# Attention, three-way maximum and gated feed-forward on one Trainium2 core: where the SBUF tiles begin, modulo 128 bytes

## The chip, the cores and the metric

One core of one Trainium2 chip runs the whole program. The metric is device time in microseconds (us), the median of several executions. Before the change it is 1110.41 us, with three runs between 1109.85 and 1111.0.

## What is computed

Inputs are float32 q, k, v of shape [4, 12, 448, 64] and five weight matrices that arrive as 8-byte floats. The reference, cut to its arithmetic:

```python
scores = q @ k.transpose(0, 1, 3, 2) / sqrt(64)
scores = cap * tanh(scores / cap)
attn = softmax(scores)
x = (attn @ v), heads joined            # [1792, 768]
h = maximum(maximum(x @ w1, x @ w2), x @ w3)   # w1..w3 [768, 768]
y = h @ w_out                           # [768, 768]
out = (silu(y @ w_gate) * (y @ w_val)) @ wo    # [768, 1536] twice, [1536, 768]
```

## The kernel before

TensorE multiplies float32 in the reduced form `float32r`. To keep the accuracy, nearly every operand is cut into a high and a low part (`parts_of`, L507: ACT or POOL copies the high part, DVE or POOL subtracts), and every product is made of three matmuls: high by high, high by low, low by high. Each matmul loads its own 128 x 128 weights (the stationary operand) and streams 448 or 384 columns (the moving operand) through them. Moving columns are 4 bytes each, so one matmul reads 1792 or 1536 contiguous bytes from every partition.

The work goes through these stages; the names are those of the trace, written out<-in.

- Attention, pairs of heads: `scores` (L217, `sc<-qh,kh` and the like), `values` (L257). For the first eight pairs `values` multiplies plain float32 (`pv<-e,vp`, moving `e`), and the trace holds two records for each such matmul. Later pairs use the parts `eh`, `el`. Transposes of q and k (L193, L207) have the identity as their moving operand.
- `x @ w1..w3` (`ff1`, L566, and `group`, L551: `ps_h<-x,ws`, 1296 matmuls, moving `x`), woven into the attention of the next batch by `weave` (L594), then alone. Meanwhile the 8-byte weights are loaded (`raw`), turned into float32 by integer arithmetic (`convert`, L468) and cut into parts (`ws`, L514) in steps given out one by one.
- `h @ w_out` (`ps_y<-ha,ws`, 432 matmuls, moving `ha`).
- `y @ w_gate` and `y @ w_val` in seven products instead of eight (`product`, L871, 1512 matmuls). Half of the moving operands lie in `yo0` (in the trace `yo`), the other half in `b11`, `yo1a`, `yo1b`, `yo1c` (in the trace `b`, `yo1a`, ...).
- the last product (`out_part`, L942: `ps_o<-wo,g`, 1008 matmuls of 384 columns, moving `wo`).

The order of the work on each engine is written out by hand (`manual_schedule`); the change leaves it as it is. What concerns the change is the memory. SBUF pools stack up from two ends of each partition: those of the default side from low addresses up, those with `side="right"` from the top (byte 229344) down. `const` (L52) is the first pool of the left side, so what it holds shifts everything that is stacked on it: `cv`, `wp`, `per`, `stk`, `ring`, `seq`, `wo` and the rest. On the right side lie `res` (with `x`), `yo0`, `yf` and `ct`.

The first tile of `const`, `ident`, begins at byte 1152 = 9 x 128. Behind it stands `four` (L54), four columns of per-partition constants, 16 bytes that take 32. Nearly all other tiles are whole multiples of 128 bytes long (the largest: 1792 = 14 x 128, 2048, 3072, 3584, 6144, 10752, 21504, 73728, 75264). So before the change every large tile on the left begins at 32 past a multiple of 128, and every large tile on the right at 96 past one, because 229344 is 1791 x 128 + 96. The start of the operands in a partition, as the built program has them:

| tile | side | before, first byte | before, modulo 128 | after, first byte | after, modulo 128 |
|---|---|---|---|---|---|
| ident | left | 1152 | 0 | 1152 | 0 |
| qn, kn | left | 1696 | 32 | 1664 | 0 |
| ws, o_A, o_S, g (weights of matmuls) | left | 22176 | 32 | 22144 | 0 |
| e, eh, el | left | 87712 | 32 | 87680 | 0 |
| ha, yo1a | left | 66720 | 32 | 66688 | 0 |
| wo (moving) | left | 55968 | 32 | 55936 | 0 |
| x | right | 127456 | 96 | 127360 | 0 |
| yo0 | right | 154080 | 96 | 153984 | 0 |
| ct, yf | right | 132576 | 96 | 132480 | 0 |

Every slice that a matmul reads lies a whole multiple of 128 bytes into its tile, or, for some weights of `pv`, a multiple of 64 bytes.

Of the kernel before, what the change touches and what calls it, by code (L numbers as in the profile page):

```python
# [9 lines left out]
F32 = mybir.dt.float32  # L10
# [14 lines left out]
@with_exitstack  # L25
def attention_max_silu_kernel(ctx, tc, q, k, v, cap, w1, w2, w3, w_out, wg, wv, wo, out):

    nc = tc.nc
    B, H, S, D = q.shape
    P = 128
    CQ = S // 4
    KL = S - 3 * P
    NP = H // 2  # L50

    const = ctx.enter_context(tc.tile_pool(name="const", bufs=1))  # L52
    ident = const.tile([P, P], F32, name="ident")
    four = const.tile([P, 4], F32, name="four")  # L54
    capt, acap, ncap, qsc = (four[:, i : i + 1] for i in range(4))


    qn = [const.tile([P, 4, 2, D], F32, name=f"qn{i}") for i in range(2)]
    kn = [const.tile([P, 4, 2, D], F32, name=f"kn{i}") for i in range(2)]

    def load_pair(g):
        load_k(g)
        load_q(g)

    def load_k(g):
        b, hp = divmod(g, NP)
        load_keys(k[b, 2 * hp : 2 * hp + 2], kn[g % 2])

    def load_q(g):
        b, hp = divmod(g, NP)  # L70
        for j in range(2):
            (nc.scalar if g < NP + 2 else nc.sync).dma_start(
                out=qn[g % 2][:CQ, :, j], in_=q[b, 2 * hp + j].rearrange("(p c) d -> p c d", c=4)
            )

    def load_keys(src, t, outside=False):


        for j in range(2):
            r = slice(j * KL, (j + 1) * KL)  # L80
            nc.sync.dma_start(
                out=t[:, j, 0:3] if outside else t[:, 0:3, j],
                in_=src[j, : 3 * P].rearrange("(p c) d -> p c d", c=3),
            )
            nc.sync.dma_start(out=t[r, j, 3] if outside else t[r, 3, j], in_=src[j, 3 * P :])

    bits = nc.values_load(cap.rearrange("(a b) -> a b", a=1).bitcast(mybir.dt.int32))
    with tc.manual_schedule(), tc.tile_pool(name="ps_w", bufs=1, space=PSUM) as ps_w:
        nc.gpsimd.memset(kn[0][:, 3], 0.0)
        nc.gpsimd.memset(kn[1][:, 3], 0.0)  # L90
        make_identity(nc, ident)
        load_pair(0)
        nc.scalar.dma_start(out=capt, in_=cap.partition_broadcast(P))
        load_pair(1)
        nc.scalar.activation(qsc, ident[:, 0:1], AF.Tanh)
        ps = ps_w.tile([P, 512], F32, name="warm")
        for i in range(24):
            nc.tensor.transpose(ps[:, i % 4 * P : (i % 4 + 1) * P], ident, ident)  # L98

    shared = dict(ident=ident, capt=capt, acap=acap, ncap=ncap, qsc=qsc, qn=qn, kn=kn, load_k=load_k, load_q=load_q, load_keys=load_keys)  # L100
    tensors = (q, k, v, w1, w2, w3, w_out, wg, wv, wo, out)
    with tc.If((bits & 0x7FFFFFFF) < 0x42000000) as bounded:
        program(tc, tensors, shared, False)
    with bounded.Else():
        program(tc, tensors, shared, True)
# [955 lines left out]
```

## Time and profile before

| | |
|---|---|
| median of 3 runs | 1110.41 us (1109.85 to 1111.0) |
| the profiled execution: span from first to last instruction | 1111.6 us |
| PE (TensorE) busy | 1075.8 us, 97% |
| DVE, POOL, ACT busy | 685.2, 658.5, 511.9 us |
| mean share of the 16 DMA engines in use | 35.6% |
| mean granted TensorE clock | 0.988 of full speed |

The profiled execution's own time is given by its span, 1.2 us above the median. PE's busy time is the union of its matmuls' spans; since they overlap in the pipeline, a busy PE can still stream slower or faster. What a stream of matmuls costs is read from the distance between starts: n matmuls in a row that are listed with a length L, of which one lasts d, start (L - d)/(n - 1) apart.

### The profile page before, as it was taken

To read this page: it belongs to the slowest core of one execution; us is meant where nothing else is said; L and a number is where in the kernel's file an instruction comes from. 1 tells how busy PE (TensorE), PEld (TensorE's weight loads), DVE (VectorE), ACT (ScalarE), POOL (GpSimd) and SP (SyncE) were. 2 spreads that over 40 slices of the span, in tenths; PEclk is the share of its full clock that TensorE was granted. 3 is DMA by queue.
4 is the path that set the end of the run, shared out by engine and by line. 5 is a ranking of instruction groups with operands and counts; after the bars stand their busy time and mean duration, and the time that the engine had idled before them with its cause. 6 is when DMAs were issued, how large, how long until landed. Compare 5 with 4: busy or idle time off the path is not lost.

```text
span 1111.6 us, 15026 instructions
## 1 busy us (share of the span) xinstructions
PE 1075.8 (97%) x5480; PEld 937.4 (84%) x5480; DVE 685.2 (62%) x884; ACT 511.9 (46%) x798; POOL 658.5 (59%) x550
## 2 busy tenths in 40 slices
PE   7986999999999999999999999999999998999998
PEld 4443778888888888999998999999999998999997
DVE  2766899957777677866547876666667645211110
ACT  4766768867677664343535433333332233212110
POOL 1356998787887879997363456655655555211210
PEclk9999999999999999999999999999999998999999
DMA  5555445433434422433212023333233228232231
GB/s 140 132 140 157 116 114 146 115 100 104 137 93 116 132 91 94 151 117 126 95 46 82 17 75 105 98 111 101 91 95 117 68 84 250 66 108 86 85 100 61
DMA packets 158531, 118.44 MB, mean 107 GB/s; under 512 B 72432, under 2 KB 153840, under 8 KB 158448
## 3 DMA queue, kind: packets, MB, share of 16 engines
q1 hardware_dynamic: 150880, 115.55, 34.6%
q10 hardware_dynamic: 7568, 1.84, 0.7%
q8 instruction: 45, 0.74, 0.3%
q14 instruction: 38, 0.31, 0.1%
HBM read 90.44 MB, written 26.82 MB: 105 GB/s over the span
## 4 chain that ended last, share of the span: by engine, by line
PE 86%; DMA 4%; DVE 3%; POOL 2%; ACT 2%; SPq 1%; issue 1%; ACTq 0%; POOLq 0%; DVEq 0%
PE ps_g L880 28%; PE ps_h L558 23%; PE ps_o L952 16%; PE pv L278 7%; PE ps_y L558 5%; PE sc L229 5%; DMA rb<-rd 1%; DMA su<-o 1%; POOL yf L728 1%; PE pq L193 1%; PE pk L207 1%; DMA rd<-rs 1%; DVE el L253 1%; DMA hr<-h 1%; PE warm L98 0%
## 5 line engine op out<-in xcount | busy, mean ns | idle before, releaser
L558 PE MATMUL ps_h<-x,ws 128*128 128x448 f32 x1296 | 287.4, 368 | 0.7 <-ACT ht L581 0.7
L558 PEld LDWEIGHTS ps_h<-x,ws 128*128 128x128 f32 x1296 | 238.6, 188 | 35.2 <-issue 17.3
L512 POOL TENSOR_TENSOR ws<-w,ws 128x384 fp32r<-128x384 f32 x144 | 181.6, 1270 | 11.6 <-ACT ws L509 4.1
L952 PE MATMUL ps_o<-wo,g 128*128 128x384 f32 x1008 | 177.9, 338 | 3.7 <-ACT g L509 2.5
L952 PEld LDWEIGHTS ps_o<-wo,g 128*128 128x128 f32 x1008 | 177.3, 190 | 4.4 <-ACT g L509 2.8
L499 POOL TENSOR_TENSOR t<-t,raw 128x768 uint32<-128x768 uint32 x42 | 82.4, 1961 | 117.0 <-DVE raw L496 108.9
L253 DVE TENSOR_TENSOR el<-e,eh 128x896 fp32r<-128x896 f32 x64 | 88.0, 1378 | 43.6 <-ACT eh L252 36.3
L243 ACT ACTIVATE e<-e,four 128x896 f32<-128x896 f32 x96 | 99.4, 1035 | 4.8 <-DMA qn<-in_q_dram 3.9
L512 POOL TENSOR_TENSOR g<-gr,g 128x384 fp32r<-128x384 f32 x28 | 32.8, 1193 | 113.4 <-ACT g L509 113.4
L235 ACT ACTIVATE e<-sc,four 128x896 f32<-128x896 f32 x96 | 86.9, 905 | 23.0 <-PE sc L229 22.9
L880 PE MATMUL ps_g<-yo,o_S 128*128 128x448 f32 x432 | 93.5, 362 | 0.0
L558 PE MATMUL ps_y<-ha,ws 128*128 128x448 f32 x432 | 90.5, 371 | 3.1 <-ACT ha L509 1.5
L558 PEld LDWEIGHTS ps_y<-ha,ws 128*128 128x128 f32 x432 | 82.2, 191 | 11.4 <-ACT ha L509 1.8
L880 PEld LDWEIGHTS ps_g<-yo,o_S 128*128 128x128 f32 x432 | 81.0, 187 | 6.0
L278 PE MATMUL pv<-eh,vs 128*128 128x448 f32 (+1 forms) x256 | 76.9, 381 | 0.0
L511 POOL TENSOR_SCALAR ws<-w 128x384 fp32r<-128x384 f32 x90 | 76.2, 847 | 0.0
L512 DVE TENSOR_TENSOR g<-gr,g 128x384 fp32r<-128x384 f32 x28 | 24.9, 899 | 74.6 <-ACT g L509 74.5
L880 PE MATMUL ps_g<-yo,o_A 128*128 128x448 f32 x324 | 70.3, 362 | 0.0
L880 PEld LDWEIGHTS ps_g<-yo,o_A 128*128 128x128 f32 x324 | 60.8, 188 | 4.5
L904 ACT ACTIVATE ct<-ct 128x448 f32<-128x448 f32 x23 | 13.3, 579 | 99.4 <-DVE ct L903 99.4
L499 POOL TENSOR_TENSOR w<-w,raw 128x768 uint32<-128x768 uint32 x18 | 36.4, 2020 | 38.0 <-DVE raw L496 38.0
L278 PE MATMUL pv<-e,vp 128*128 128x448 f32 (+1 forms) x128 | 53.7, 592 | 3.9 <-ACT o L296 2.6
(135 smaller groups left out, 1872.2 us busy)
## 6 DMA issues: line engine op xcount, KB each, us to landing
raw<-in_moe_w_dram SPq DMA_DIRECT2D x18, 768.0 KB, 4.6
raw<-in_moe_w_out_dram SPq DMA_DIRECT2D x18, 768.0 KB, 4.8
gr<-gd SPq DMA_DIRECT2D x14, 768.0 KB, 5.2
raw<-in_moe_w_gate_dram SPq DMA_DIRECT2D x12, 768.0 KB, 4.7
raw<-in_moe_w_val_dram SPq DMA_DIRECT2D x12, 768.0 KB, 4.6
rb<-rd SPq DMA_DIRECT2D x48, 112.0 KB, 3.0
h<-ht SPq DMA_DIRECT2D x24, 224.0 KB, 2.0
hr<-h SPq DMA_DIRECT2D x24, 224.0 KB, 2.7
```

Source lines behind the costliest of these rows:

```text
L229: nc.tensor.matmul(ps[:, j, :S], a[r, cols_], m[r], start=i == 0, stop=i == 2)
L235: nc.scalar.activation(ee[n][:, :w], ps[:, :w, :S], AF.Tanh, scale=qsc)
L243: nc.scalar.activation(t, t, AF.Exp, bias=ncap, scale=acap)
L253: nc.vector.tensor_sub(lo, t, f(hi))
L278: nc.tensor.matmul(pv[g][j][:, :S], a, m, start=c == 0 and x == 0, stop=c == 3 and x == len(ops) - 1,)
L499: nc.gpsimd.tensor_tensor(t, t, low, op=ALU.add)
L511: copier.tensor_scalar(hi, src, 1.0, 1.0, ALU.mult, ALU.mult)
L512: subtracter.tensor_tensor(lo, src, f(hi), op=ALU.subtract)
L558: nc.tensor.matmul(ps, a, m, start=kk == 0 and n == 0, stop=kk == NK - 1 and n == 2)
L880: nc.tensor.matmul(ps, a[:, s0, k3], m[:, kk, s1], start=kk == 0 and j == 0, stop=kk == 2 and j == 2,)
L904: nc.scalar.activation(t[0], t[0], AF.Silu)
L952: nc.tensor.matmul(po[s][x][:, :HW], a, m[:, x * HW : (x + 1) * HW], start=c == 0 and n == 0, stop=c == NF2 - 1 and n == 2,)
```

## The change

`four` leaves the pool `const` and gets a pool of its own, `top`, the first on the right side, with 24 columns (96 bytes) instead of 4. The four columns that are used stay the first four. The 96 bytes reach from 229248 to the top, so that the pools below begin at 229248 = 1791 x 128; on the left `qn` follows `ident` directly. On every engine and every DMA queue the instructions, their order and their waits are the same as before, and so are the PSUM banks and the DRAM scratch tensors.

```diff
     const = ctx.enter_context(tc.tile_pool(name="const", bufs=1))
     ident = const.tile([P, P], F32, name="ident")
-    four = const.tile([P, 4], F32, name="four")
+    top = ctx.enter_context(tc.tile_pool(name="top", bufs=1, side="right"))
+    four = top.tile([P, 24], F32, name="four")
     capt, acap, ncap, qsc = (four[:, i : i + 1] for i in range(4))
```

## Rows read from the trace of the kernel before

**Rows 1.** The page's busy times by engine.
```profile
PE 1075.8 (97%) x5480; PEld 937.4 (84%) x5480; DVE 685.2 (62%) x884; ACT 511.9 (46%) x798; POOL 658.5 (59%) x550
```

**Rows 2.** The page's chain that ended last, by engine and by line.
```profile
PE 86%; DMA 4%; DVE 3%; POOL 2%; ACT 2%; SPq 1%; issue 1%; ACTq 0%; POOLq 0%; DVEq 0%
PE ps_g L880 28%; PE ps_h L558 23%; PE ps_o L952 16%; PE pv L278 7%; PE ps_y L558 5%; PE sc L229 5%; DMA rb<-rd 1%; DMA su<-o 1%; POOL yf L728 1%; PE pq L193 1%; PE pk L207 1%; DMA rd<-rs 1%; DVE el L253 1%; DMA hr<-h 1%; PE warm L98 0%
```

**Rows 3.** Windows by stage: length, busy us of each engine, granted clock, DMA share, GB/s.
```profile
175.00:425.00 250.00, 250.00 (x1336) 207.64 (x1335) 188.20 (x218) 177.65 (x231) 202.45 (x185) 1.00 0.38 113
425.00:525.00 100.00, 98.59 (x493) 91.09 (x492) 73.99 (x77) 38.99 (x78) 92.81 (x74) 1.00 0.37 119
525.00:608.00 83.00, 80.63 (x387) 73.56 (x386) 43.71 (x57) 39.03 (x74) 36.50 (x27) 0.98 0.26 84
608.00:935.00 327.00, 323.31 (x1579) 298.00 (x1579) 226.51 (x340) 110.74 (x207) 188.31 (x148) 0.99 0.30 95
935.00:1112.00 177.00, 171.31 (x988) 170.99 (x986) 30.06 (x41) 31.27 (x66) 33.67 (x27) 0.99 0.32 95
```

**Rows 4.** Timeline of PE, 690 to 698 us: start, us, instructions merged.
```profile
690.33 1.96 PE L880 MATMUL ps_g<-yo,o_S 128*128 128x448 f32 x9
692.13 2.02 PE L880 MATMUL ps_g<-yo1c,o_S 128*128 128x448 f32 x9
693.99 1.96 PE L880 MATMUL ps_g<-yo,o_A 128*128 128x448 f32 x9
```

**Rows 5.** Timelines of PE in four long runs of matmuls without a gap.
```profile
449.81 24.36 PE L558 MATMUL ps_h<-x,ws 128*128 128x448 f32 x121
...
540.74 20.23 PE L558 MATMUL ps_y<-ha,ws 128*128 128x448 f32 x99
...
603.69 8.63 PE L558 MATMUL ps_y<-ha,ws 128*128 128x448 f32 x41
...
955.69 140.56 PE L952 MATMUL ps_o<-wo,g 128*128 128x384 f32 x810
```

**Rows 6.** Groups by shape: busy us, mean ns of one, idle before.
```profile
L880 PE MATMUL ps_g<-yo,o_S 128*128 128x448 f32 x432 | 93.5, 362 | 0.0
...
L278 PE MATMUL pv<-eh,vs 128*128 128x448 f32 x192 | 63.4, 371 | 0.0
```

**Rows 7.** Timeline of PE near 40 us: plain float32, two passes; and one run of it.
```profile
39.60 1.29 PE L278 MATMUL pv<-e,vp 128*128 128x448 f32 x3
...
54.32 0.54 PE L278 MATMUL pv<-e,vp 128*128 128x448 f32 x1
```

**Rows 8.** Window of L558 alone where the granted clock is 0.50.
```profile
597.50:600.50 3.00, 3.00 (x9) 2.65 (x9) 0.50 0.00 0
```

**Rows 9.** Windows of one line's matmuls: L558 (three windows), then L278, then L229.
```profile
0.00:175.00 175.00, 33.51 (x145) 26.50 (x146) 0.96 0.51 134
175.00:425.00 250.00, 158.81 (x682) 124.23 (x682) 1.00 0.38 113
425.00:525.00 100.00, 95.69 (x475) 88.42 (x474) 1.00 0.37 119
...
175.00:425.00 250.00, 63.39 (x301) 47.33 (x300) 1.00 0.38 113
...
175.00:425.00 250.00, 42.38 (x261) 25.34 (x261) 1.00 0.38 113
```

**Rows 10.** Windows of 25 us in which another engine comes near its limit.
```profile
450.00:475.00 25.00, 25.00 (x126) 23.43 (x125) 18.98 (x19) 11.89 (x26) 24.42 (x19) 1.00 0.43 137
600.00:625.00 25.00, 25.00 (x123) 22.92 (x122) 22.42 (x29) 13.45 (x28) 12.75 (x10) 0.99 0.10 32
```

**Rows 11.** Same addition on a right tile (ct) and on a left one (kn).
```profile
L900 DVE TENSOR_TENSOR ct<-ps_g,ct 128x448 f32<-128x448 f32 x23 | 14.3, 621 | 6.2 <-PE ps_g L880 6.1
L896 DVE TENSOR_TENSOR kn<-ps_g,ct 128x448 f32<-128x448 f32 x13 | 8.1, 622 | 7.0 <-PE ps_g L880 7.0
```

## The prediction, made before the changed kernel was run

> **What bounds the kernel now.** The busy times come first: PE is busy for 97% of the span, the next engine for 62% [rows 1]. The chain that ended last says the same with the waits followed back: 86% of it is PE, and five lines of matmuls carry nearly all of that [rows 2]. By stage, PE has no gap from 175 to 425 us and few after it; the one stage in which another engine is close behind is 425 to 525, where POOL is busy 92.81 of 100 us [rows 3]. So the kernel ends sooner only if PE's streams get shorter. The change takes no instruction away: orders, waits, PSUM and DRAM are what they were. It can only act through the place of the operands, so the question is whether a place already shows in the pace of the matmuls.
>
> It does. From 690 to 698 us PE does nothing but runs of nine matmuls of one kind [rows 4]. Runs whose moving operand is `yo` (right side, 96 past a multiple of 128) take 692.13 - 690.33 = 1.80 us, 200.0 ns for each matmul. Runs of the same shape that read `yo1c` (left side, 32 past a multiple) take 693.99 - 692.13 = 1.86 us, 206.7 ns. Weights (all left), PSUM banks and columns are alike; only the place of the moving operand differs. The long runs give the pace elsewhere [rows 5]: `x` (right, 96) (24.36 - 0.36)/120 = 200.0 ns; `ha` (left, 32) (20.23 - 0.37)/98 = 202.7 ns, and later (8.63 - 0.37)/40 = 206.5 ns; `wo` (left, 32, 384 columns) (140.56 - 0.33)/809 = 173.3 ns. [...]
>
> [...] A run of 1792 bytes that starts at 96 touches 15 blocks of 128 bytes, and one of 1536 bytes that starts at 32 touches 13. [...] I take it that the supply comes in blocks of 128 bytes and that a run which starts inside one pays for one more; the rest on the left I read as a stall that depends on the offset.
>
> **The change part by part.** With every start at 0 a run of 1792 bytes touches 14 blocks, one of 1536 touches 12: as much as the array consumes. [...]
>
> The gain by stage, matmuls times distance saved, against the span of 1111.6 us:
> - 0 to 175 us: PE often waits for loads and for the sums, so a shorter stream is mostly answered by a longer wait. 145 `ps_h` [rows 9] and a few others start here, 3 us of stream at most; I count 0.6.
> - 175 to 425: 682 of `ps_h` [rows 9] by 11.3 ns, 7.7 us. Its 301 `pv` by 14.0 (`eh` shows 371 ns each against 362 for `yo`, so a left pace [rows 6]) would be 4.2 us and its 261 `sc` 3.7, but many of these run two at a time on half the rows each; I count half, 3.9. Together 11.6, taken as 11.5. The others have 250 us for 202 of POOL and 188 of DVE [rows 3], so nothing is in the way.
> - 425 to 525: 475 matmuls of L558 [rows 9] by 11.3, 5.4 us of stream. POOL's 92.81 us stay, with 24.42 of 25 in the densest window [rows 10]; it cuts the `ws` that PE waits for. I count about half, 2.6.
> - 525 to 608: PE's 387 matmuls [rows 3], all on `ha`, by 14.0 ns, 5.4, less 0.4 for PE's idle time there, which can grow. 5.0.
> - 608 to 935: 1512 `ps_g`, half by 11.3 and half by 18.0: 8.5 + 13.6 = 22.1. DVE has 226.51 us of 327, but 22.42 of 25 at the start [rows 3, 10], for which I take 1.1 off. 21.0.
> - 935 to 1112: 1008 `ps_o` by 11.3, 11.4, less 0.9 for the waits before the stage fills. 10.5.
>
> The sum is 51.2 us: 1111.6 - 51.2 = 1060.4 for a profiled execution. The span stands 1.2 us above the median, so the median comes to 1059.2.
>
> What is at nothing: DVE, ACT and POOL. The same addition takes 621 ns on `ct` (96) and 622 on `kn` (32) [rows 11]; both places are off 128, so a gain is not excluded, but these engines are hidden behind PE, and a loss has no row that speaks for it. `four` itself is read by the activations from another address, at the pace of a scalar per partition; nothing. DMA carries 4% of the chain, 44 us [rows 2]. One block more or less in fifteen would be 3 us either way; I take 0 and keep 3 for the range's upper end, since the lower one already takes everything as given.
>
> If everything is given (2 ns more on each of some 4,600 matmuls, all stages in full, 58 + 9 us) the median is 1043; that is the lower end. If POOL keeps 425 to 525 as it is and half of 175 to 425 is lost, 51.2 - 2.6 - 5.7 = 43 leaves 1067. With the 3 us for DMA on that side the forecast's own range is 1043 to 1070.
>
> **The rivals.**
> 1. *Others take over.* PE gets its pace, but POOL, DVE and the chains of the conversions hold the woven stages: nothing before 525 us and 70% of `ps_g`: 5 + 15 + 10.5 = 31 us, 1079. For it speaks the density of POOL [rows 10], against it 81% and less in the other stages [rows 3].
> [...]
> 3. *It doesn't do what it says.* The difference in rows 4 may come from the side (bytes below or above some place) and not from the remainder; left and right stay as they are: no change, 1110. [...]
> 4. *A low start is dear.* Going from 96 to 32 costs 6.7 ns. If the cost rises as the offset falls, 0 is no better than 32, and the 1296 matmuls on `x` and the 756 on `yo` lose what `ps_g` shows for the left: 2052 x 6.7 = 13.7 us, 1124. It decides from the point where a run of nine from `yo` takes 1.86 us or more. Against it: a start at a block's edge is the one place with no part block.
>
> **How the numbers follow.** The forecast has 0.62, others take over 0.11, the fixed step 0.08, no change 0.10, a low start 0.09. The time is the forecast's, 1059. The first three make 0.81, so the range runs from 1043 to 1104; the forecast's own is 1043 to 1070. About 0.2% is what a measurement of this kernel tells from no change. Faster by more than that are the forecast, others take over and the fixed step, 0.81; within it 0.10; slower 0.09.
>
> **What would show it.** In the timeline of PE the runs of nine from `yo` and from `yo1c` should take the same 1.70 us; the long runs of `x` and `ha` should go at 188 to 189 ns, that of `wo` at 162, while the plain `pv` stays at 375. The stage of `ps_o` should be shorter by 10 us or more, and POOL above 95% from 425 to 520. PE's busy share falls a little, as its waits grow. Wrong is the forecast if the run of nine from `yo` stays at 1.80 (2 or 3) or rises (4); right in mechanism but mis-sized if the pace falls and the span falls by less than 40 us (1).

## The result, and the profile after

The changed kernel is slower. Its median is 1118.14 us over 13 runs (1112.90 to 1125.61), that of the kernel before, on the same chip, 1111.29 us over 13 runs (1109.85 to 1114.53). The ratio is 1.0054, with a 95% interval from 1.0029 to 1.0078, so between 3 and 9 us were lost where 51 were forecast as a gain. The profiled execution has a span of 1116.3 us, 4.7 above that of before.

The page's busy times of the changed kernel, which answer to [rows 1], and its chain that ended last, which answers to [rows 2]:

```profile
PE 1081.0 (97%) x5480; PEld 940.1 (84%) x5480; DVE 680.4 (61%) x884; ACT 511.8 (46%) x798; POOL 651.8 (58%) x550
...
PE 85%; DMA 4%; DVE 4%; POOL 2%; ACT 2%; issue 1%; SPq 0%; ACTq 0%; POOLq 0%; DVEq 0%
PE ps_g L881 27%; PE ps_h L559 23%; PE ps_o L953 16%; PE pv L279 7%; PE ps_y L559 5%; PE sc L230 5%; DMA raw<-in_moe_w_dram 1%; POOL yf L729 1%; PE pq L194 1%; DVE el L254 1%; PE pk L208 1%; DMA su<-o 1%; DMA kn<-in_k_dram 1%; DVE xp L328 1%; PE warm L99 0%
```

Nothing has taken over from PE: its busy time grew by 5.2 us, that of DVE and POOL fell by 5 to 7. The windows by stage, with the columns of [rows 3], say where PE is full:

```profile
0.00:175.00 175.00, 151.98 (x685) 95.43 (x685) 120.36 (x152) 111.15 (x139) 98.75 (x90) 0.94 0.51 133
175.00:425.00 250.00, 250.00 (x1334) 206.25 (x1335) 183.62 (x217) 178.77 (x234) 199.62 (x183) 1.00 0.39 113
425.00:525.00 100.00, 99.97 (x493) 91.28 (x492) 75.53 (x78) 41.05 (x81) 91.18 (x74) 1.00 0.40 123
608.00:935.00 327.00, 323.35 (x1592) 299.16 (x1591) 225.83 (x342) 112.34 (x212) 188.73 (x149) 1.00 0.31 96
```

From 175 to 525 us PE is busy all the time, from 425 on with not even the 1.4 us of idle time it had before, so it has become more of a bound there and not less. The timeline of PE over the stretch of [rows 4]:

```profile
691.37 1.99 PE L881 MATMUL ps_g<-yo,o_A 128*128 128x448 f32 x9
693.19 1.99 PE L881 MATMUL ps_g<-yo1c,o_A 128*128 128x448 f32 x9
695.01 1.98 PE L881 MATMUL ps_g<-yo,o_S 128*128 128x448 f32 x9
696.83 1.99 PE L881 MATMUL ps_g<-yo1c,o_S 128*128 128x448 f32 x9
```

Nine matmuls now take 1.82 us, 202.2 ns each (202.7 as a mean over the whole stage), whichever of the two tiles they read. Before they took 1.80 on `yo` and 1.86 on `yo1c` [rows 4]. So the runs did become alike, but between the old two values, not 11 to 18 ns below them. The long runs, against [rows 5]:

```profile
439.58 40.61 PE L559 MATMUL ps_h<-x,ws 128*128 128x448 f32 x199
...
539.81 58.94 PE L559 MATMUL ps_y<-ha,ws 128*128 128x448 f32 x290
...
999.77 110.58 PE L953 MATMUL ps_o<-wo,g 128*128 128x384 f32 x637
```

`x` goes at (40.61 - 0.37)/198 = 203.2 ns where it went at 200.0, `ha` at (58.94 - 0.36)/289 = 202.7 as before, and `wo` at (110.58 - 0.33)/636 = 173.3, as before to a tenth. Every one of these starts is now a multiple of 128 bytes.

Where the 4.7 us of the profiled span arise, by the starts of single matmuls in the two timelines: 3.7 before the 175th `ps_h` (which starts at 189.0 us instead of 185.3), 1.2 from there to the first `ps_g`, -1.0 in the stage of `ps_g`, 0.1 in that of `ps_o`, 0.6 behind it. The first part is no more than executions differ by, whatever the kernel: in the nine profiles of whole kernels (these two and the seven below), that 175th start lies anywhere from 183.7 to 189.0 us, at 185.3 and 186.8 in two of the kernel before and at 189.0 and 185.1 in two of the changed one. So one pair of profiles does not show the loss stage by stage; what differs steadily is the pace of `x` and `yo`.

### The profile page after: what moved, and what is told of

Read it like the earlier page. It is cut to its first block, busy times and chain, and to the rows that moved or that the text cites. A ratio compares the mean times of both kernels' runs of the same rounds, so it can differ in the third digit from the quotient of the medians.

```text
span 1116.3 us, 15026 instructions
## 1 busy us (share of the span) xinstructions
PE 1081.0 (97%) x5480; PEld 940.1 (84%) x5480; DVE 680.4 (61%) x884; ACT 511.8 (46%) x798; POOL 651.8 (58%) x550
## 3 DMA queue, kind: packets, MB, share of 16 engines
q10 hardware_dynamic: 7568, 1.84, 0.7%
## 4 chain that ended last, share of the span: by engine, by line
PE 85%; DMA 4%; DVE 4%; POOL 2%; ACT 2%; issue 1%; SPq 0%; ACTq 0%; POOLq 0%; DVEq 0%
PE ps_g L881 27%; PE ps_h L559 23%; PE ps_o L953 16%; PE pv L279 7%; PE ps_y L559 5%; PE sc L230 5%; DMA raw<-in_moe_w_dram 1%; POOL yf L729 1%; PE pq L194 1%; DVE el L254 1%; PE pk L208 1%; DMA su<-o 1%; DMA kn<-in_k_dram 1%; DVE xp L328 1%; PE warm L99 0%
## 5 line engine op out<-in xcount | busy, mean ns | idle before, releaser
L559 PE MATMUL ps_h<-x,ws 128*128 128x448 f32 x1296 | 291.4, 372 | 0.0
L513 POOL TENSOR_TENSOR ws<-w,ws 128x384 fp32r<-128x384 f32 x144 | 178.6, 1248 | 16.6 <-ACT ws L510 9.1
```

The costliest lines, as they stand in the source:

```text
L513: subtracter.tensor_tensor(lo, src, f(hi), op=ALU.subtract)
L559: nc.tensor.matmul(ps, a, m, start=kk == 0 and n == 0, stop=kk == NK - 1 and n == 2)
```

## The experiments

What both kernels share besides the pace is a number that the prediction did not look at. Before, weights lie at 32, `yo` and `x` at 96, `yo1c`, `ha` and `wo` at 32. So the slow left tiles are not only at another offset: they lie a whole multiple of 128 from the weights that are loaded beside them, and the fast right ones 64 from such a multiple. The change puts all of them at a whole multiple. The theory to test is that this distance, moving start minus weights' start, sets the pace. Its rivals are that an offset as such does (a start at 0, or a side, is dear), and that the pace differs from one execution to the next and places do nothing.

Eleven kernels ran, on three chips; each time is compared with the kernel before on the same chip. Each pace below is the mean distance between the starts of neighbouring matmuls at the full clock, over a whole profile or a whole series.

**1. Only the right side at 64 (right64).** `four` gets 8 columns, so that the right side lies at 64 and the left stays at 0.

```diff
-    four = top.tile([P, 24], F32, name="four")
+    four = top.tile([P, 8], F32, name="four")
```

> Four has 8 columns, so the right tiles (x, yo) begin at 64 past a multiple of 128, the left tiles and all weights at 0. Theory A (distance: the pace of a full-clock float32r matmul depends on the distance of its moving run from its weights, modulo 128; 64 apart gives 200.0 ns, 0 apart gives 202.7 or 206.7): ps_h on x and ps_g on yo at 200.0 ns, ps_y on ha and ps_g on yo1 at 202.7 or 206.7 as in both kernels; time as before the change, 1109 to 1114 us. Theory B (start: a run that begins at a multiple of 128 is itself the dear one): the same for x and yo; it differs in the next kernel. Theory C (chance: the paces are drawn anew in each run, whatever the place): x and yo at 202 to 207 as often as not, 1113 to 1125 us.

Measured: 1111.47 us over 12 runs against 1111.14 of before, ratio 1.0001 (0.9980 to 1.0022). The loss is gone. In its timeline of PE `yo` is faster than its neighbours again:

```profile
690.69 1.97 PE L881 MATMUL ps_g<-yo,o_S 128*128 128x448 f32 x9
692.50 1.99 PE L881 MATMUL ps_g<-yo1c,o_S 128*128 128x448 f32 x9
694.32 1.97 PE L881 MATMUL ps_g<-yo,o_A 128*128 128x448 f32 x9
```

A run on `yo` has 1.81 us to the next, one on `yo1c` 1.82; over the stage 200.9 and 202.7 ns. `x` goes at 200.8. Offset 64 does as well as 96 did, so it is not the old offset that was good.

**2. Everything at 32 (both32).** Distance 0 as in the changed kernel, but no start at 0.

```diff
     ident = const.tile([P, P], F32, name="ident")
+    const.tile([P, 8], F32, name="pad")
     top = ctx.enter_context(tc.tile_pool(name="top", bufs=1, side="right"))
-    four = top.tile([P, 24], F32, name="four")
+    four = top.tile([P, 16], F32, name="four")
```

> Four has 16 columns and a pad of 32 bytes stands behind ident, so both sides begin at 32 past a multiple of 128: nothing is aligned, yet moving runs and weights are 0 apart everywhere. Theory A: no tile at 200.0, all 448-column streams at 202.7 or 206.7, time as after the change, 1113 to 1126 us. Theory B: no start at 0, so the gain of the old places comes back: x and yo at 200.0, 1109 to 1114 us.

Measured: 1114.96 us over 12 runs (1110.97 to 1123.36), ratio 1.0040 (1.0013 to 1.0066): slower, like the changed kernel. From its timeline of PE:

```profile
692.88 2.02 PE L882 MATMUL ps_g<-yo1c,o_A 128*128 128x448 f32 x9
694.74 2.02 PE L882 MATMUL ps_g<-yo,o_S 128*128 128x448 f32 x9
696.60 2.02 PE L882 MATMUL ps_g<-yo1c,o_S 128*128 128x448 f32 x9
```

1.86 us for each run, 206.7 ns, `yo` like `yo1c`. So a start at 0 is not what costs. The same kernel reads `x` at 202.7 and `ha` first at 202.7 and, after a stretch of longer distances (33 matmuls in 8.52 us from 599.78 us on; the mean granted clock of 525 to 608 us is 0.98), at 206.7 (61 in 12.77 us from 607.73 on): at distance 0 there are at least two paces, and a stream changes from one to the other without any change of place.

**3. Offsets and column counts by themselves (offsets).** A kernel of matmuls alone, in series of 54, whose moving tile and weights start at chosen offsets; the starts alternate by 128 bytes:

```python
a = w0 // 4 + i % weights * 128
b = m0 // 4 + i % 2 * 32
nc.tensor.matmul(ps[:wide, :cols], wt[:, a : a + wide], mv[:, b : b + cols], ...)
```

> Computes nothing of the reference: only streams of 54 float32r matmuls, 448 columns, 128 weights, on one tile, at given starts modulo 128 of the moving run (d) with weights at 0. Series pa to ph are d = 0, 16, ... 112, qa to qh the same again, ra to re (64,64), (0,64), (32,32), (96,32), (32,96) for moving and weights, sa to sf d = 0 with 512, 384, 320, 256, 192, 128 columns, ta to tf d = 64 with the same, ua to uc d = 0 with 96, 64, 32 weights columns, va to vc d = 64 with the same, wa and wb one and the same weights at d = 0 and 64. Theory A: pe, qe, rb, rd, re at 200.0 ns (64 apart), pa, qa, ra, rc at 202.7 or 206.7. Theory B: pa, qa and rb dear, ra and rc cheap. [...]

Measured: all eight offsets go at 203.0 to 204.6 ns and none at 200.0, which neither the theory nor the rivals gave. Experiment 7 shows a part of the reason: two starts 128 apart are not equivalent, and these series mix them. It is not all of it, since the paces found there for distances of 64 and 192 have a mean of 201.2 and the mixed series takes 203.3. What the kernel does settle is what depends on the columns. Timeline of PE, a series of 54 with distance 0 for each count:

```profile
267.83 12.58 PE L41 MATMUL sa<-mv,wt 128*128 128x512 f32 x54
...
292.73 9.61 PE L41 MATMUL sb<-mv,wt 128*128 128x384 f32 x54
...
311.54 8.08 PE L41 MATMUL sc<-mv,wt 128*128 128x320 f32 x54
...
327.38 6.57 PE L41 MATMUL sd<-mv,wt 128*128 128x256 f32 x54
...
396.93 10.96 PE L41 MATMUL vb<-mv,wt 128*64 128x448 f32 x54
...
418.53 11.14 PE L41 MATMUL vc<-mv,wt 128*32 128x448 f32 x54
```

The paces are 230.0, 174.9, 146.7 and 118.7 ns, which is 0.449, 0.455, 0.458 and 0.464 ns a column; in the same series with the moving start at 64 they are 231.0, 173.5, 146.7 and 116.7 ns, 0.451 to 0.458 a column. The forecast's 188 to 189 ns for 448 columns and 162 for 384 would be 0.42 a column, and no column count comes down to that, though the series with distance 0 all start at a multiple of 128. The last two lines, `vb` and `vc`, have the moving start at 64 and weights of only 64 and 32 columns: 200.1 and 203.3 ns. With 128 columns of weights the same starts give 203.3, so from these starts fewer columns of weights to load took off 3.2 ns at 64 columns and nothing at 32.

**4. Does a pace last? (gaps).** The same streams eight times over, with pauses of 2.5 us between.

> Computes nothing of the reference: eight times the same four series at the full clock, p (moving 0 apart from the weights, 60 matmuls), q (64 apart), r and s (384 columns, 0 and 64 apart), then PE waits some 15 to 25 us for GpSimd, the granted clock falls, and series t warms it again. Theory A: all q at 200.0 and s at 173.3 ns; p the same inside one stretch of full clock and either 202.7 or 206.7 (perhaps others) from stretch to stretch, changed by the fall of the clock; r at 173.3. Theory C: q changes from stretch to stretch as p does.

Measured: with the moving start at 64, 203.2 ns in all eight stretches (the expected 200.0 was missed, as at 3); at 0, 204.3 in seven and 203.3 in one; at 384 columns 173.2 at 64 and 175.2 at 0. The waits for GpSimd were 2.5 us and not 15 to 25, and after seven of the eight the first matmuls were 373 ns apart (`tb` to `th`, 60 matmuls each, take 13.76 to 13.89 us, `ta` 12.47; the mean granted clock of the run is 0.96). A pause did not change a pace here, apart from that one stretch.

**5. Every distance at 64 (all64).** `right64`, and a 64-byte pad behind the pool `wp`, which holds the weights, and one ahead of `cv1`. Then `x`, `yo`, `b`, `yo1a` to `yo1c` and `wo` lie 64 from their weights, and so do `eh` and `el`; only `ha` with the weights in `wp2`, and the products of q and k, stay at distance 0.

```diff
-    four = top.tile([P, 24], F32, name="four")
+    four = top.tile([P, 8], F32, name="four")
...
     wp = ctx.enter_context(tc.tile_pool(name="wp", bufs=8))
+    ctx.enter_context(tc.tile_pool(name="gap", bufs=1)).tile([P, 16], F32, name="gap")
...
     per = pool(att_pools, "per", 1)
+    pool(att_pools, "gap2", 1).tile([P, 16], F32, name="gap2")
```

> As the kernel with the right tiles at 64, and two pads of 64 bytes on the left, so that ha, b, yo1, wo and x, yo all lie 64 from the weights in wp, and eh, el 64 from vs; only q/k and a third of ps_y's weights (those in wp2) stay 0 apart. Theory A (distance of moving run and weights modulo 128 sets the pace): every 448-column stream of the long stages at 200 to 201 ns, none at 202.7 or 206.7; against the kernel before that is 756 left ps_g by 2 to 6 ns, some 290 ha by 2 to 6 and the pv by 2: 3 to 7 us, 1104 to 1109 us, ratio 0.994 to 0.998. Theory C (the pace is drawn at each start of a stream, whatever the place): some of these streams at 202.7 or 206.7, time as before, ratio 0.998 to 1.004.

Measured: 1106.67 us over 12 runs (1104.42 to 1112.72) against 1111.26 of before, ratio 0.9971 (0.9951 to 0.9991). It is faster than both kernels. Timeline of PE:

```profile
690.22 1.96 PE L883 MATMUL ps_g<-yo1c,o_S 128*128 128x448 f32 x9
692.02 1.96 PE L883 MATMUL ps_g<-yo,o_A 128*128 128x448 f32 x9
693.82 1.96 PE L883 MATMUL ps_g<-b,o_A 128*128 128x448 f32 x9
695.62 1.96 PE L883 MATMUL ps_g<-yo,o_S 128*128 128x448 f32 x9
```

1.80 us for every run, left or right: 200.0 ns. Within one line of the program, `ha` goes at 200.1 with weights in `wp`; with those in `wp2` it goes at 202.7 in the first two banks of 18 matmuls and at 206.7 in the six later ones, on the same moving tile. That is the distance at work, with the offset of the moving start unchanged.

**6. The kernel's own order of reads (pattern).** Series of 54 as in 3, but with the strides of `product`: moving starts 1792 bytes apart, weights 512, both multiples of 256.

```python
a = w0 // 4 + s0 * 384 + kk * 128
b = m0 // 4 + (kk * 2 + s1) * cols
```

> Computes nothing of the reference: streams of 54 matmuls in the order and the strides of product() (weights high, high, low; moving high, low, high, 1792 bytes apart), at full clock, six times (a to f) the same set: p to w with the moving run at 0, 16, 32, 48, 64, 80, 96, 112 and weights at 0; x (96, weights 32), y (32, weights 32), z (0, weights 64), m and n the moving run in the right half of SBUF at 0 and 64, h and k 384 columns at 0 and 64. Between the sets PE waits for ACT, after a and d long for GpSimd. Theory A: t, x, z, n at 200 to 201 ns in all six sets, p, y, m at 202.7 to 206.7, which may change from set to set; h and k at 173.3. Theory B (a start at 0 is itself dear): z as p, y as t. Theory C: no order by place, changes from set to set. Side: m and n differ from p and t.

Measured, weights at 0, timeline of PE (`pa` to `wa` have the moving start at 0, 16, ... 112; `xa` is moving 96 with weights 32, `ya` 32 with 32; `ma` and `na` lie on the right side at 0 and 64):

```profile
37.10 11.11 PE L47 MATMUL pa<-ml,wt 128*128 128x448 f32 x54
48.05 10.96 PE L47 MATMUL qa<-ml,wt 128*128 128x448 f32 x54
...
80.85 10.97 PE L47 MATMUL ta<-ml,wt 128*128 128x448 f32 x54
...
113.71 11.29 PE L47 MATMUL wa<-ml,wt 128*128 128x448 f32 x54
124.84 10.97 PE L47 MATMUL xa<-ml,wt 128*128 128x448 f32 x54
135.64 11.32 PE L47 MATMUL ya<-ml,wt 128*128 128x448 f32 x54
...
157.71 11.11 PE L47 MATMUL ma<-mr,wt 128*128 128x448 f32 x54
168.65 10.97 PE L47 MATMUL na<-mr,wt 128*128 128x448 f32 x54
...
371.23 11.22 PE L47 MATMUL pc<-ml,wt 128*128 128x448 f32 x54
```

Paces: 202.6 at 0, 200.1 at 16, 204.5 at 32, 202.9 at 48, 200.2 at 64, 203.2 at 80, 205.3 at 96, 206.2 at 112. Moving 96 with weights at 32 gives 200.1, and 32 with 32 gives 206.7, the two paces of [rows 4]. The right side repeats the left: 202.6 and 200.2. So sides do nothing, and an offset only through its distance: 96 is slow against weights at 0 and fast against weights at 32. In six sets each of them repeats within 0.1 ns. Three series of moving 0 with weights 0 are 0.11 us longer (`pc` in the last line), but that is a single start, 311 ns after the first one, behind the step on ScalarE between the sets; the rest of them goes at 202.6 as in the other three. The six sets run in one order, so their agreement does not exclude that a series takes over a pace from the one before it; experiment 7 has another order. At 384 columns these two distances make no difference: 173.4 at 0 and 173.3 at 64, and `wo` never moved.

**7. Distance beyond 128 (map256).** The same series with moving starts from 0 to 240, equal distances at other places, and two series with 2-byte elements (bfloat16).

> Computes nothing of the reference: streams of 54 matmuls in the order of product(), at the full clock, twice (a, b): ad to pd with the moving run at 0, 16, ... 240 and weights at 0, then as to hs with moving and weights at (32,32), (64,64), (96,96), (96,32), (128,64), (160,96), (0,64), (128,192), then ahalf and bhalf with 2-byte elements (bf16) at 0 and 64. Theory A (distance modulo 128): id to pd repeat ad to hd (md, 192, at 200 as ed, 64), gs and hs at 200. Theory D (distance modulo 256, 64 past is good, 192 past is not): md, gs and hs near 202.2 as z of the pattern, ds, es, fs at 200.1. Theory E (which of the two leads decides, not the modulus): md at 200, gs and hs at 202. The place alone adds something if as, bs, cs differ from ad (206.7 at 32 and 202.6 at 0 in the pattern). [...]

Measured, timeline of PE (`eda` moving 64 with weights 0; `kda` 160 with 0; `mda` 192 with 0; `asa` 32 with 32; `dsa`, `esa`, `fsa` distance 64 at three places; `gsa` moving 0 with weights 64; `ahalfa` 2-byte elements):

```profile
80.77 10.97 PE L51 MATMUL eda<-ml,wt 128*128 128x448 f32 x54
...
146.94 10.97 PE L51 MATMUL kda<-ml,wt 128*128 128x448 f32 x54
...
168.78 11.08 PE L51 MATMUL mda<-ml,wt 128*128 128x448 f32 x54
...
212.70 11.11 PE L51 MATMUL asa<-ml,wt 128*128 128x448 f32 x54
...
245.54 10.96 PE L51 MATMUL dsa<-ml,wt 128*128 128x448 f32 x54
256.34 10.97 PE L51 MATMUL esa<-ml,wt 128*128 128x448 f32 x54
267.15 10.97 PE L51 MATMUL fsa<-ml,wt 128*128 128x448 f32 x54
277.96 11.07 PE L51 MATMUL gsa<-ml,wt 128*128 128x448 f32 x54
...
299.80 10.39 PE L51 MATMUL ahalfa<-mb,wb 128*128 128x448 bf16 x54
```

Distance 64 gives 200.2, distance 192 gives 202.3, so 128 bytes apart is not the same place; 160 gives 200.1, 128 gives 203.8 and 144 gives 206.5. Distance 64 gives 200.0 to 200.2 at each of three places, and moving 0 with weights 64 (192 modulo 256) gives 202.1, as moving 192 with weights 0 does. So for these the distance modulo 256 counts, and not the place. Distance 0 has no one pace: 32 with 32, at 206.7 in all sets of experiment 6, goes at 202.7 here in both sets. The second set of the same series repeats the first within 0.3 ns but for its first three, which follow the step on ScalarE between the sets (206.7 at 0 behind its first starts, 202.2 at 16 instead of 200.1, 206.4 at 32 instead of 204.5). So at the same places another pace can hold for whole series. The 2-byte series takes (10.39 - 0.35)/53 = 189.4 ns, and 189.2 with the moving start at 64. No float32r series of 448 columns on all 128 partitions came below 199.9 in this case.

**8. The two kernels once more (before2, after2).** Unchanged, one run each on the chip of 5 and 6, to see which paces belong to the kernel and which to the execution.

> The kernel before once more. Theory A: x and yo at 200 to 201 ns as in its first profile; ha and yo1 at 202.7 or 206.7, not necessarily in the same stages. Theory C: x or yo at 202 to 207 as well.

> The changed kernel once more, to see how its paces change from one execution to the next. Theory A: x, yo, ha and yo1 at 202 to 207 ns, not all at the paces of its first profile; none steadily at 200. Theory C: some stage at 200.0.

Measured: 1110.65 and 1112.58 us. The kernel before shows `x` at 200.6 and `yo` at 200.9, near the 200.7 and 199.9 of its first profile, but `yo1c` at 202.7 instead of 206.7. Its timeline of PE:

```profile
690.90 1.99 PE L880 MATMUL ps_g<-yo1c,o_S 128*128 128x448 f32 x9
692.73 1.97 PE L880 MATMUL ps_g<-yo,o_A 128*128 128x448 f32 x9
694.54 1.99 PE L880 MATMUL ps_g<-b,o_A 128*128 128x448 f32 x9
```

So a good part of the 6.7 ns of [rows 4] belonged to that execution and not to the place. The changed kernel shows 202.7 on all four kinds. What repeats is that a tile 64 away is at 200.0 to 200.9 and a tile at distance 0 at 202.7 or more.

**9. 192 against 64 in the whole kernel (apart192, apart64far).** `right64` with the left side moved down by 128 bytes and by 256, through the scratch area ahead of it. All offsets modulo 128 are those of `right64`; the distance of `x` and `yo` is 192 in the first and 64 in the second (modulo 256).

```diff
-    four = top.tile([P, 24], F32, name="four")
+    four = top.tile([P, 8], F32, name="four")
...
-    nc = _bacc.Bacc("TRN2", target_bir_lowering=False, num_devices=1, dynamic_dma_scratch_size=1024)
+    nc = _bacc.Bacc("TRN2", target_bir_lowering=False, num_devices=1, dynamic_dma_scratch_size=896)
```

(`apart64far` has 768 in that place.)

> The kernel with four of 8 columns (right tiles at 64) and the scratch at the bottom of SBUF 128 bytes shorter, so that all left tiles move by 128: still 64 modulo 128 from weights to x and yo, but 192 modulo 256. Theory A: x and yo at 200 to 201 ns, time as the kernel before (1108 to 1113 us, ratio 0.997 to 1.002). Theory D: x and yo at 202 to 203 ns or more, time as after the change (1111 to 1120 us, ratio 1.001 to 1.007).

> The same with the scratch 256 bytes shorter: the distance is 64 modulo 256 again, and everything on the left has moved by 256. Theories A and D: x and yo at 200 to 201 ns, ratio 0.997 to 1.002. If moving the left side does something by itself, this one shows it.

Measured: 1112.79 us (1110.74 to 1115.90), ratio 1.0014 (0.9998 to 1.0029), and 1111.74 us (1109.09 to 1115.89), ratio 1.0005 (0.9988 to 1.0021). The times alone do not tell them apart. The paces do: `x` 202.0 and `yo` 201.8 at 192, 200.8 and 200.9 at 64, in the order of the series of 7 (202.3 and 200.2).

All whole kernels together; the last but one column is the stream time of 1296 matmuls on `x`, 756 on `yo` and 756 on the left half, at these paces, and the time is the median where several runs were made:

| kernel | distance of x, yo (modulo 256) | of the left half | x, ns | yo, ns | left half, ns | sum, us | us |
|---|---|---|---|---|---|---|---|
| before | 64 | 0 | 200.7 | 199.9 | 206.7 | 567.5 | 1111.3 |
| before, once more | 64 | 0 | 200.6 | 200.9 | 202.7 | 565.1 | (1110.7, one run) |
| changed | 0 | 0 | 203.2 | 202.7 | 202.7 | 569.8 | 1118.1 |
| changed, once more | 0 | 0 | 202.7 | 202.7 | 202.7 | 569.1 | (1112.6, one run) |
| both32 | 0 | 0 | 202.7 | 206.7 | 206.7 | 575.1 | 1115.0 |
| apart192 | 192 | 0 | 202.0 | 201.8 | 206.4 | 570.4 | 1112.8 |
| right64 | 64 | 0 | 200.8 | 200.9 | 202.7 | 565.4 | 1111.5 |
| apart64far | 64 | 0 | 200.8 | 200.9 | 202.7 | 565.3 | 1111.7 |
| all64 | 64 | 64 | 200.7 | 200.0 | 200.0 | 562.5 | 1106.7 |

The two kernels that are slower than before (`changed` and `both32`) and `apart192`, whose interval just includes 1, have the three largest sums, and the fastest has the smallest. The order among the slow ones is not that of the sums, since a sum is of one execution and at distance 0 the paces change between executions.

## Why the prediction was wrong

**What bounds the kernel: right.** PE is busy 97% of the time in both, and its streams set the end. A pace that rose by 1% reached the time.

**The reading in blocks: wrong, and this is the step that failed.** "I take it that the supply comes in blocks of 128 bytes and that a run which starts inside one pays for one more." For it spoke that 200.0 ns over 15 blocks and 173.3 over 13 are both 13.33 ns a block. With every start at the edge of such a block the paces are 202.7, 203.2 and 173.3 ns instead of the 188 to 189 and 162 forecast. The whole numbers were a coincidence of two column counts: at 512, 320 and 256 columns, from starts at 0, the distances are 230.0, 146.7 and 118.7 ns, which is 17.25, 11.0 and 8.9 times 13.33 ns, where an aligned run touches 16, 10 and 8 blocks. What the runs do show is where 448 columns go relatively faster: at a granted clock of 0.50 the matmuls of `ha` start 373 ns apart (eight distances in 2.99 us, in the stretch of [rows 8]), 1.81 to 1.84 times the 206.5 and 202.7 of [rows 5] and not twice; and 2-byte elements go at 189.2 to 189.4 ns (experiment 7). No place tried brought float32r matmuls of 448 columns on all 128 partitions below 199.9 ns (`el` in `all64`). Why that is so is not shown.

**The left surplus: wrong cause.** "The rest on the left I read as a stall that depends on the offset." It depends on the distance from the weights, modulo 256 bytes (experiments 5 to 7, 9), and at distance 0 on the execution too (202.7 or 206.7, experiment 8). [Rows 4] held offset and distance changed together, and the sentence "only the place of the moving operand differs" overlooked that a place can matter relative to another.

**The sum.** All terms rest on 11.3, 14.0 and 18.0 ns per matmul, which suppose an aligned matmul at 188.7 ns (162.0 for `wo`), and the range's lower end supposes 2 ns less. No run shows such a pace; in its place the changed kernel's streams went at 202.7, 203.2 and 173.3 ns. So `x` lost 2.5 ns on 1296 matmuls, 3.2 us; `yo` lost 2.7 on 756, 2.1 us; the left half gained 4.0 on 756, 3.0 us, in these two profiles, and nothing against the second profile of before. That is 2.3 us by the first and 4.7 by the second (569.8 - 565.1), where the median shows 6.9 and the interval reaches down to 3.2. So these terms account for the sign and, within the interval, for most of the size. The rest lies within what executions of the changed kernel differ by (1112.9 to 1125.6), and which stage it falls in is not shown, since timed runs leave no trace. The stages on `ha` and `wo`, priced at 5.0 and 10.5 us, gave nothing: their paces are the old ones. The terms of all stages in full add to 60.5 us and not to the 58 of the range's lower end; that moves only an end that was not reached.

**The terms at nothing: right.** The addition on `ct` takes 620 ns, on `kn` 622, against [rows 11]. The DMA's share of the chain is 4% as before.

**The rivals.** *A fixed step*, that a stream keeps its pace wherever it starts and only the surplus of the left tiles can go, has 0.08 and takes the range up to 1104. The left half did gain 3.0 us in this profile, and `wo` stayed at 173.3 ns; but `x` and `yo`, which by it keep their pace, lost 5.3. *A low start is dear* gave the right sign and 13.7 us of loss, with a run from `yo` at 1.86 us; the run took 1.82 and the loss was half of that. The sign is luck, as the reason is refuted: `both32` has no start at 0 and loses too, and in `all64` `el`, at offset 0, goes at 199.9 ns where it went at 203.8 from offset 32. *It doesn't do what it says* set on the side; the right side repeats the left (experiment 6). *Others take over* was not reached.

## What to carry to other kernels

When two streams differ in pace, list every place that differs between them, and the places of one operand relative to the other, before giving the difference to one; here one micro-series with weights and moving tile shifted separately would have told them apart in advance. On this chip, with 448 float32r columns, put the moving tile 64 bytes from its weights modulo 256: a pad of 64 bytes in the pool between them was worth 0.3% (ratio 0.9971, 0.9951 to 0.9991), and alignment for its own sake, which brought the distances to 0, cost 0.5%. Whole multiples read from two paces (15 and 13 blocks) are weak evidence until a third size has been measured.

## What was not expected of the hardware

- The pace of float32r matmuls of 448 columns depends on the distance of moving start and weights' start modulo 256 bytes: 200.0 to 200.2 ns at 64 and 160 (at 16 too, but for one series at 202.2), 202.1 to 202.3 at 192, 206.2 to 206.5 at 112 and 144. At 384 columns distances 0 and 64 gave the same (173.3 to 173.4) in the kernel's own order of reads; in the alternating starts of experiments 3 and 4 they differed there too (174.9 to 175.2 against 173.2 to 173.5). What ties the pace to the distance is not shown.
- At distance 0 a stream of the kernel goes at about 202.7 or 206.7 ns, keeps one for hundreds of matmuls, and took the other after short waits and 33 matmuls in 8.52 us (`ha` in `both32`: 202.7, then 206.7) or after a stretch at a granted clock of 0.50 (`ha` of before: 202.7, then 206.5). What chooses between them is not shown. At distance 64 `x` and `yo` stay within 199.9 to 200.9 in the five profiles that have it. Whether these paces make the scatter of the times is not shown: the changed kernel's runs span 12.7 us against 4.7 of before in the same comparison, but those of before span 11.9 (1106.6 to 1118.5, 23 runs) beside `right64`.
- The time of a column falls a little with their number: 0.456 to 0.464 ns at 256 columns and 0.449 to 0.451 at 512 (experiment 3). At 448, float32r takes 0.446 or more (199.9 ns) and 2-byte elements 0.422 (189.2 ns); what makes the difference stays open. Below 256 columns the pace hardly falls any more: 111.2 ns at 192 and at 128 columns alike, with the moving start at 0.
